# A convolution stem's forward and backward pass: every engine's order of work read from a fixed list

## The chip, the cores and the metric

The kernel runs on one core of a Trainium2 chip. A core has five engines that run at the same time, each in its own strict order of instructions: PE (TensorE, the matmuls; PEld are its weight loads), DVE (VectorE), ACT (ScalarE), POOL (GpSimd) and SP (SyncE, which here issues the transfers between HBM and on-chip memory). Sixteen DMA engines carry those transfers. An instruction starts when the one before it on its engine lets it and when the semaphores it waits for have come. The metric is device time in microseconds (us) of one execution; lower is better.

## What is computed

```python
def _fwd_reference(x, w, gn_gamma, gn_beta):     # x 2x16000x256, w 31x256x256
    s = 2
    L = (T - K) // s + 1                          # 7985
    h = jnp.einsum('blc,cd->bld', x[:, 0:s * L:s, :], w[0])
    for i in range(1, K):
        h = h + jnp.einsum('blc,cd->bld', x[:, i:i + s * L:s, :], w[i])
    mu = jnp.einsum('bld->bd', h)[:, None, :] / L
    var = jnp.einsum('bld->bd', (h - mu) ** 2)[:, None, :] / L
    h = (h - mu) / jnp.sqrt(var + 1e-5)
    h = h * gn_gamma[None, None, :] + gn_beta[None, None, :]
    return _gelu(h)

def reference(x, w, gn_gamma, gn_beta, grad_out):
    _out, _vjp = jax.vjp(_f, x, w, gn_gamma, gn_beta)
    return (_out, *_vjp(grad_out))
```

So it is a 31-tap convolution of stride 2 over 256 channels, a normalisation over time for each channel, a gelu, and then the gradients with respect to x, w, gamma and beta. All arrays are bf16.

## The kernel before

**Three convolutions as matmuls.** The forward pass (about 4 to 390 us, `f_mm`, line 815), the gradient of x (about 390 to 819 us, `g_mm`, line 1363) and the gradient of w (about 820 us to the end, `w_mm`, line 1653) are each a convolution. Each is made with fewer multiplications by splitting the taps and the positions into three branches, called A, B_ and C_ in the code, at several levels: DVE forms sums and differences of inputs and weights (`w_sub` 768, `tt` 783 and 1326, `w_add` 1616, `w_two` 1607, `pair_d` 1712), PE multiplies them, and ACT and DVE take the results out of PSUM and join them (`keep` 868, `f_evac` 890, `f_join` 917, `g_join` 1405, `w_sum` 1659). PSUM is a ring of four tiles, `ps0` to `ps3`, so a group of matmuls cannot begin in a tile until ACT or DVE has emptied it.

**Stages.** The forward pass goes over 2 batches (b) of 4 chunks (c) of time, and in each over the branches B_, A, C_. A chunk's x is brought in transposed into the one tile `XT` by four transfers (`x_load`, 713; the first chunk also through PE, `x_first`). Its h goes into the one tile `HS` (`f_evac`), and from there to HBM in one store of 1 MB (line 914). The elementwise part (normalisation, gelu, its derivative) runs under the matmuls of the second batch and of the first chunk of the x gradient. In the x gradient, DVE also forms differences of the gradient for the last stage (`d2_piece`, 1533), which go out to HBM and come back in the weight gradient (`d_tile`, 1641). That last stage has nine rounds n = 0 to 8; each takes four tiles of x (`x_tile`, 1625, through `x_raw`, 1618), two of differences (`D2`), forms `pair_x`, `leaf_d` and `pair_d` on DVE, and multiplies.

**What sets the order.** The program is not emitted as it is written. Every operation is recorded by `plan.add` with its engine, its assumed duration, its inputs and outputs, and is given a number in the order of recording; 3164 operations are recorded (900 groups of matmuls on PE, 994 on DVE, 721 on ACT, 23 on POOL, 526 transfers on SP). `Plan.order` then works out one list of all numbers, by due times taken backwards from the matmuls, a table of corrections by kind of operation (`self.lead`), and two rounds of a simulated run (`listing`, `latest`). `Plan.emit` (516) emits the operations in that list's order, and the framework keeps that order on every engine and puts in the semaphores. All transfers of more than 4 KB go through the one queue of SP (`load`, 602; `turn`, 612, for transposing ones). SP waits for what a transfer needs before it issues it, and what stands behind it on SP waits too.

**Tiles that the change moves.** In odd rounds of the weight gradient the four x tiles lie in `XT_` (line 1579), in even ones in `XS_`. `pair_x` and others take two tiles of the two batches as one operand through `both` (1598) where they lie near enough.

Of the kernel before, what the change touches and what calls it, by code (L numbers as in the profile page):

```python
# [37 lines left out]

class Plan:
# [3 lines left out]
    def __init__(self, tc):  # L43
# [10 lines left out]
        self.lead = {  # L54
            "F0 conv_stem_kernel wrapper": 5.6,
            "F0 f_evac last": -3.2,
            "F0 f_join f_evac": -10.3,
            "F0 f_join split": 14.0,
            "F0 f_mm f_three_ac": -0.4,
            "F0 f_mm f_three_b": 1.0,  # L60
            "F0 f_three_b split": -3.7,
            "F0 keep f_evac": -3.1,
            "F0 keep split": -17.8,
            "F0 load conv_stem_kernel": 58.4,
            "F0 load f_evac": -14.0,
            "F0 load put": 0.6,
            "F0 load x_pre": 3.5,
            "F0 load_gb conv_stem_kernel": -25.1,
            "F0 tt f_sums": -15.0,
            "F0 tt second": 4.0,  # L70
            "F0 tt third": -5.9,
            "F0 turn w2_part": -0.5,
            "F0 turn x_load": -4.6,
            "F0 w_sub w2_part": -5.7,
            "F0 x_pre conv_stem_kernel": 1.3,
            "F0 zero conv_stem_kernel": 0.9,
            "F0 zero f_evac": -7.8,
            "F0 zero w2_part": -33.8,
            "F0 zero x_load": -111.5,
            "F0a f_evac last": -19.8,  # L80
            "F0a f_join f_evac": 0.7,
            "F0a f_join f_first": -11.0,
            "F0a f_join split": 28.3,
            "F0a f_mm f_leaf": -8.4,
            "F0a f_mm f_three_ac": 0.2,
            "F0a f_mm f_three_b": -5.0,
            "F0a f_mm pe_turn": -48.4,
            "F0a f_three_b f_first": -12.7,
            "F0a f_three_b split": -30.8,
            "F0a keep f_first": -31.2,  # L90
            "F0a keep split": -10.0,
            "F0a load load_w": 58.4,
            "F0a load x_load": 82.3,
            "F0a load x_pre": 55.5,
            "F0a put x_first": -19.2,
            "F0a tt f_sums": -12.3,
            "F0a tt second": -19.7,
            "F0a tt third": -13.9,
            "F0a turn x_load": -48.2,
            "F0a w_sub f_first": -12.5,  # L100
            "F0a x_pre conv_stem_kernel": 13.3,
            "F0a zero load_w": 14.3,
            "F1 f_evac last": 4.0,
            "F1 f_join f_evac": 11.4,
            "F1 f_mm f_leaf": 0.7,
            "F1 f_mm f_three_b": 1.8,
            "F1 f_three_b plain": -0.7,
            "F1 f_three_b split": -2.0,
            "F1 gelu_batch conv_stem_kernel": -6.7,
            "F1 gelu_unit gelu_batch": 0.7,  # L110
            "F1 keep f_evac": -0.4,
            "F1 keep plain": -0.3,
            "F1 keep split": -34.2,
            "F1 load f_evac": 0.5,
            "F1 load gelu_unit": 3.0,
            "F1 load out0_store": -3.7,
            "F1 tiny elem_finalize": -260.7,
            "F1 tiny fwd_stats": 2.5,
            "F1 tt f_sums": -15.6,
            "F1 tt second": -1.3,  # L120
            "F1 tt third": 0.6,
            "F1 turn gelu_batch": 0.5,
            "F1 turn gelu_unit": 3.7,
            "F1 turn x_load": 1.8,
            "F1 zero gelu_batch": -52.4,
            "F1z f_evac last": -7.1,
            "F1z f_join f_evac": -5.3,
            "F1z f_join split": -17.5,
            "F1z f_mm f_leaf": -2.5,
            "F1z f_mm f_three_ac": 0.6,  # L130
            "F1z f_mm f_three_b": -0.3,
            "F1z f_three_b split": 2.4,
            "F1z keep f_evac": 7.0,
            "F1z keep split": -160.7,
            "F1z load f_evac": 7.0,
            "F1z tt f_sums": -20.3,
            "F1z tt second": -3.1,
            "F1z tt third": -0.7,
            "F1z turn x_load": 8.8,
            "F1z w_sub f_again": -0.3,  # L140
            "F1z zero f_evac": -10.2,
            "F1z zero x_load": -6.0,
            "G0 e_add e_comp": 3.6,
            "G0 e_comp conv_stem_kernel": -3.2,
            "G0 e_spread conv_stem_kernel": 8.2,
            "G0 g_join last": 1.0,
            "G0 g_mm g_leaf": -0.9,
            "G0 g_mm g_three_ac": 0.8,
            "G0 g_mm g_three_b": 0.7,
            "G0 g_three_b plain": 1.3,  # L150
            "G0 g_three_b split": 5.1,
            "G0 keep last": 1.4,
            "G0 keep plain": 4.1,
            "G0 keep split": -156.4,
            "G0 load dn_turn": 15.0,
            "G0 load e_load": -6.2,
            "G0 spread e_spread": -288.3,
            "G0 tt first": -2.4,
            "G0 tt outer": 17.1,
            "G0 tt second": -7.8,  # L160
            "G0 tt third": 14.0,
            "G0 turn dn_turn": -10.7,
            "G0 zero e_comp": -37.5,
            "G0 zero e_spread": 69.3,
            "G0a e_add e_comp": -0.5,
            "G0a e_comp conv_stem_kernel": -5.0,
            "G0a e_spread conv_stem_kernel": -1.4,
            "G0a g_join last": -0.9,
            "G0a g_mm g_leaf": 1.6,
            "G0a g_mm g_three_ac": 2.7,  # L170
            "G0a g_mm g_three_b": 2.3,
            "G0a g_three_b plain": 0.6,
            "G0a gelu_batch conv_stem_kernel": -22.1,
            "G0a gelu_unit gelu_batch": 0.3,
            "G0a keep last": 3.8,
            "G0a keep plain": -2.4,
            "G0a load dgb_store": 91.4,
            "G0a load dn_turn": -2.4,
            "G0a load e_load": 11.2,
            "G0a load g_store": 9.1,  # L180
            "G0a load gelu_unit": 4.5,
            "G0a load load_w2": -6.9,
            "G0a spread e_spread": -45.7,
            "G0a tiny elem_finalize": -2.2,
            "G0a tiny fwd_stats": -186.8,
            "G0a tt first": 20.5,
            "G0a tt gelu_unit": -0.6,
            "G0a tt second": -4.2,
            "G0a tt third": 1.7,
            "G0a turn dgb_store": -3.7,  # L190
            "G0a turn gelu_batch": -1.8,
            "G0a w_sub w2_sub": 2.0,
            "G0a zero conv_stem_kernel": -104.8,
            "G0a zero e_spread": -148.7,
            "G0a zero gelu_batch": -5.4,
            "G1 e_add e_comp": -0.5,
            "G1 e_comp conv_stem_kernel": 1.5,
            "G1 e_spread conv_stem_kernel": 0.2,
            "G1 g_join last": 1.0,
            "G1 g_join split": 4.3,  # L200
            "G1 g_mm g_three_ac": -2.1,
            "G1 g_mm g_three_b": -0.3,
            "G1 g_three_b split": -150.3,
            "G1 keep last": -1.0,
            "G1 keep split": 1.0,
            "G1 load d2_piece": 0.8,
            "G1 load dn_turn": -4.2,
            "G1 load e_load": -1.5,
            "G1 spread e_spread": 0.2,
            "G1 sub d2_piece": 0.3,  # L210
            "G1 tt first": 2.1,
            "G1 tt outer": 6.2,
            "G1 tt second": 7.7,
            "G1 tt third": 8.8,
            "G1 turn dn_turn": 0.4,
            "G1 zero e_comp": -0.2,
            "G1 zero e_spread": -0.6,
            "G1z g_join last": -4.0,
            "G1z g_join split": -7.1,
            "G1z g_mm g_three_b": 4.9,  # L220
            "G1z g_three_b split": 5.3,
            "G1z keep split": 7.7,
            "G1z load g_store": 15.8,
            "G1z tt first": -1.8,
            "G1z tt outer": 23.1,
            "G1z tt second": -0.8,
            "G1z tt third": -0.3,
            "W keep w_done": -6.2,
            "W keep weight_grad": -417.1,
            "W leaf_d weight_grad": -3.3,  # L230
            "W load d_tile": 1.3,
            "W load w_done": -3.6,
            "W load w_out": 16.2,
            "W load weight_grad": -11.1,
# [96 lines left out]
    def order(self):  # L331
# [3 lines left out]
        for i, o in enumerate(ops):  # L335
            for p in o["preds"]:
                succ[p].append(i)
# [1591 lines left out]
```

## Time and profile before

| what | us |
|---|---|
| median of 3 runs | 1110.25 |
| the three runs | 1110.12, 1110.25, 1116.37 |
| the profiled execution, its own time | 1114.1 |
| its span, first to last instruction | 1112.1 |
| first matmul starts | 4.49 |

The profile is of one execution. Its own time is 1114.1 us, 2.0 us more than its span, and 3.85 us above the median of the runs. "Waits" tells how long an engine sat idle and which instruction ended that idle time; a line number there is that of a helper, so many operations share one. The timeline merges neighbouring instructions of one line: its columns are start, duration, engine, line, operation, output and input, count, and in brackets the idle time before it. The table of stretches gives for each engine the busy time and the number of instructions in a stretch, the granted PE clock, the mean busy share of the DMA engines and GB/s.

### The profile page before, as it was taken

What the parts mean: (1) busy time and instruction counts of PE and PEld (TensorE: products, weight loads), DVE (VectorE), ACT (ScalarE), POOL (GpSimd) and SP (SyncE); (2) the same over time, 40 slices, a digit from 0 to 9 for tenths busy, and PEclk for the clock granted to TensorE, in tenths of its full rate; (3) what the DMA queues carried; (4) which work ended last, traced back from release to release, by engine and by line L of the source; (5) the groups of instructions that cost most, each with busy time, mean ns of one, the idle gap of its engine ahead of it and who ended that gap; (6) DMA issues with size and microseconds to landing.
All of it is one profiled execution on the core that took longest, in us unless ns stands there. A gap on an engine that the chain in (4) does not pass through costs nothing. (4 is left out here: it accounts for less than half of the span.)

```text
span 1112.1 us, 19739 instructions
## 1 busy us (share of the span) xinstructions
PE 1082.7 (97%) x8132; PEld 796.3 (72%) x8132; DVE 993.1 (89%) x1026; ACT 609.6 (55%) x854; POOL 11.0 (1%) x27
## 2 busy tenths in 40 slices
PE   5999999999999999999999998999999999999998
PEld 4888889988888984444444443444468888888887
DVE  6995958789998997999999979979689989999996
ACT  2253434588887659797866766665642323322332
POOL 0000000000000000000000000000000000000000
PEclk9999999999999999999999999999999999999999
DMA  9589999976969799889775999999789555796883
GB/s 227 66 220 225 242 272 272 253 151 167 190 202 186 204 334 313 203 254 276 191 245 159 280 330 295 289 301 311 247 277 270 181 194 146 262 333 205 277 255 101
DMA packets 346893, 261.47 MB, mean 235 GB/s; under 512 B 187702, under 2 KB 315572, under 8 KB 340916
## 3 DMA queue, kind: packets, MB, share of 16 engines
q1 hardware_dynamic: 346612, 260.22, 83.8%
q8 instruction: 63, 1.03, 0.4%
q14 instruction: 26, 0.21, 0.1%
q0 software_dynamic: 192, 0.00, 0.0%
HBM read 120.00 MB, written 94.86 MB: 193 GB/s over the span
## 5 line engine op out<-in xcount | busy, mean ns | idle before, releaser
L815 PE MATMUL ps<-arena 128*128 128x256 bf16 (+3 forms) x3668 | 397.7, 272 | 14.6 <-DMA arena<-in_x_dram 6.2
L1363 PE MATMUL ps<-arena 128*128 128x512 bf16 (+1 forms) x1872 | 401.0, 376 | 6.3 <-ACT arena L868 6.1
L815 PEld LDWEIGHTS <-arena 128*128 128x128 bf16 x3668 | 359.9, 99 | 52.2 <-DMA arena<-in_x_dram 6.4
L1363 PEld LDWEIGHTS <-arena 128*128 128x128 bf16 x1872 | 183.2, 98 | 223.8 <-issue 8.9
L868 ACT ACTIVATE arena<-ps 128x1024 bf16<-128x1024 f32 x189 | 191.7, 1022 | 238.8 <-PE ps L1653 123.2
L1653 PE MATMUL ps<-arena 128*128 128x256 bf16 x2592 | 284.2, 273 | 4.3 <-DVE arena L1607 4.3
L1653 PEld LDWEIGHTS <-arena 128*128 128x128 bf16 x2592 | 253.2, 98 | 35.5 <-DVE arena L1607 5.0
L783 DVE TENSOR_TENSOR arena<-arena 128x2064 bf16<-128x2064 bf16 (+7 forms) x132 | 164.7, 1270 | 24.6 <-PE ps L815 19.1
L1607 DVE TENSOR_TENSOR arena<-arena 128x4096 bf16<-128x4096 bf16 (+2 forms) x50 | 107.5, 2178 | 2.7 <-DMA arena<-d2d 2.7
L1167 DVE TENSOR_TENSOR arena<-arena 128x2048 bf16<-128x2048 bf16 (+1 forms) x80 | 95.6, 1198 | 8.9 <-ACT arena L1159 4.6
L1326 DVE TENSOR_TENSOR arena<-arena 128x1032 bf16<-128x1032 bf16 (+7 forms) x111 | 86.4, 803 | 6.7 <-PE ps L1363 5.1
L1390 ACT ACTIVATE ps<-ps 128x512 f32<-128x512 f32 x108 | 63.1, 587 | 34.8 <-PE ps L1363 34.6
L1616 DVE TENSOR_TENSOR arena<-arena 128x4096 bf16<-128x4096 bf16 x32 | 72.6, 2296 | 5.4 <-DMA arena<-in_x_dram 4.0
L1155 ACT ACTIVATE arena<-arena,stats 128x1024 bf16<-128x1024 bf16 (+1 forms) x64 | 75.1, 1209 | 0.8 <-DVE stats L1101 0.8
L1405 DVE TENSOR_TENSOR arena<-arena 128x1024 bf16<-128x1024 bf16 (+1 forms) x70 | 63.3, 919 | 7.1 <-ACT arena L868 7.0
L1549 DVE TENSOR_TENSOR arena<-arena 128x1536 bf16<-128x1536 bf16 (+3 forms) x56 | 61.9, 1128 | 8.0 <-DMA d2d<-arena 5.4
L844 ACT ACTIVATE ps<-ps 128x512 f32<-128x512 f32 x59 | 34.4, 583 | 62.1 <-PE ps L815 62.0
L1725 ACT COPY ps<-ps 128x512 f32<-128x512 f32 x54 | 30.8, 570 | 64.9 <-PE ps L1653 64.9
L1712 DVE TENSOR_TENSOR arena<-arena 128x2048 bf16<-128x2048 bf16 x54 | 64.8, 1232 | 1.1 <-DMA arena<-d2d 1.1
L768 DVE TENSOR_TENSOR arena<-arena 128x2048 bf16<-128x2048 bf16 (+1 forms) x45 | 50.8, 1151 | 16.4 <-DMA arena<-in_w_dram 9.6
L890 ACT ACTIVATE arena<-ps 128x512 bf16<-128x512 f32 (+1 forms) x64 | 36.8, 582 | 37.5 <-PE ps L815 27.7
L1659 DVE TENSOR_TENSOR arena<-arena 128x1024 bf16<-128x1024 bf16 x75 | 49.6, 699 | 6.8 <-ACT arena L868 6.8
(68 smaller groups left out, 464.3 us busy)
## 6 DMA issues: line engine op xcount, KB each, us to landing
arena<-in_x_dram SPq DMA_DIRECT2D x28, 1024.0 KB, 9.5
arena<-d2d SPq DMA_DIRECT2D x16, 1216.0 KB, 8.1
out_dram<-arena SPq DMA_DIRECT2D x35, 512.0 KB, 4.6
d2d<-arena SPq DMA_DIRECT2D x30, 384.0 KB, 6.2
arena<-dnd SPq DMA_DIRECT2D x10, 960.0 KB, 6.4
arena<-vl SPq DMA_DIRECT2D x9, 1024.0 KB, 12.2
arena<-in_x_dram SPq DMA_DIRECT2D x32, 256.0 KB, 4.4
hd<-arena SPq DMA_DIRECT2D x8, 1024.0 KB, 5.6
```

What stands on the lines that cost most here:

```text
L783: lambda: nc.vector.tensor_tensor(out=o, in0=a, in1=b, op=ALU.add))
L815: yield nc.tensor.matmul(ps[:, dh, cs], lhsT=wt, rhs=mv, start=s0, stop=False, skip_group_check=True)
L868: lambda: nc.scalar.activation(out=out, in_=ps, func=ACT.Copy, scale=scale))
L1155: lambda o=o, func=func, i=h[:, dh], sc=sc, bi=bi: SC.activation(out=o, in_=i, func=func, bias=bi, scale=sc))
L1167: add("DVE", dve(8 * wd), [o], [a, b_], lambda: V.tensor_tensor(out=o, in0=a, in1=b_, op=op))
L1326: lambda: nc.vector.tensor_tensor(out=o, in0=a, in1=b, op=ALU.add))
L1363: yield nc.tensor.matmul(ps[:, e, 0:wide], lhsT=lt, rhs=mv, start=s0, stop=False, skip_group_check=True)
L1405: add("DVE", dve(o.free_size(), rate), [o], [a, b], lambda: nc.vector.tensor_tensor(out=o, in0=a, in1=b, op=op))
L1607: add("DVE", dve(o.free_size()), outs, ins, lambda: nc.vector.tensor_tensor(out=o, in0=a, in1=b, op=op), kind=kind + " weight_grad")
L1616: add("DVE", dve(4096), [o], [a, b], lambda: nc.vector.tensor_tensor(out=o, in0=a, in1=b, op=ALU.add))
L1653: yield nc.tensor.matmul(ps[:, s, c0:c1], lhsT=lt, rhs=mv, start=s0, stop=False, skip_group_check=True)
L1712: add("DVE", dve(2048), [d4], [d], lambda: nc.vector.tensor_tensor(out=d4, in0=fan(d[:, o0:o0 + 3 * s + 1:s, :], 1, (o1 - o0) * D), in1=fa ...
```

## The change

No operation is added, removed or resized. Three things are different.

1. `Plan.order` no longer works anything out: it reads the list `STEPS`, whose running sum gives the operations' numbers in the order of emission (1, 7, 12, 6, 8, 22, 0, 9, ...). The table of corrections and the simulated run are gone.
2. The second and third of the four tiles of `XT_` change places, so that the two batches' tiles of one kind, (0, 1) with (1, 1) and (0, 0) with (1, 0), lie side by side.
3. What the planner records of dependences is a little coarser for operands of more than two strides, and a two-tile operand is recorded as one. With a fixed list this has no part in the order.

```diff
@@ -34,6 +34,85 @@
+STEPS = (
+    "1 6 5 -6 2 14 -22 9 1 -5 8 -11 22 -20 -1 23 -15 14 -2 13 -5 1 -5 6 2 -6 10 1 1 -7 13 -32 27 -4 -1 11 -5 -29 30 1 1 5 -2 -21 22 10 -30 -14 36 11 -46 "
...
+)
@@ class Plan @@
-        self.lead = {
-            "F0 conv_stem_kernel wrapper": 5.6,
...
-        }
     def order(self):
-        ops = self.ops
-        n = len(ops)
...
-        self.listing(due, succ)
-        for _ in range(self.rounds):
-            due = [d - self.lead.get(o["kind"], 0.0) for d, o in zip(self.latest(succ), ops)]
-            self.listing(due, succ)
-        return sorted(range(n), key=lambda i: (self.start[i], i))
+        steps = [int(x) for x in "".join(STEPS).split()]
+        out, at = [], 0
+        for d in steps:
+            at += d
+            out.append(at)
+        assert sorted(out) == list(range(len(self.ops)))
+        return out
...
-    XT_ = [sb(o, 8, 512) for o in (24576, 32768, 40960, 49152)]
+    XT_ = [sb(o, 8, 512) for o in (24576, 40960, 32768, 49152)]
...
-            one(both(outs), both(as_), both(bs), list(outs), ins)
+            o, a, b = (both(v) for v in (outs, as_, bs))
+            one(o, a, b, [o], [a, b])
```

Set against the order before, the list gives this (a place is an operation's rank on its own engine):

| engine | operations | at another place | moved by 5 or more | farthest |
|---|---|---|---|---|
| PE | 900 | 619 | 113 | 10 |
| DVE | 994 | 854 | 213 | 44 |
| ACT | 721 | 520 | 75 | 21 |
| POOL | 23 | 4 | 0 | 1 |
| SP | 526 | 429 | 73 | 38 |

The moves that are spoken of below, with the number of the operation, and its places before and after:

| operation | engine | what it is | place before | place after |
|---|---|---|---|---|
| 14, 15 | SP | weight loads of the first difference | 3, 4 | 10, 9 |
| 24, 26, 25, 23, 27, 29 | SP | other weight loads | 6, 11, 7, 5, 8, 10 | 2, 3, 5, 6, 7, 8 |
| 57 | DVE | the first difference of weights (`f_first`, 1015) | 7 | 11 |
| 84, 85, 86, 87, 94 | PE | leaf matmuls of the first branch, and the next group | 20, 22, 24, 28, 27 | 19, 20, 21, 22, 23 |
| 88 | PE | `f_three_b` of the first branch | 19 | 24 |
| 64, 81, 80 | DVE | sums of x for the first branch | 11, 9, 12 | 21, 23, 24 |
| 355 | SP | store of h of chunk (0, 1), 1 MB | 98 | 78 |
| 327, 352 | DVE | the joins that it waits for | 102, 104 | 97, 96 |
| 414, 415 | ACT | first writes of the next h into the same tile | 69, 70 | 68, 69 |
| 452 | PE | the group that needs the PSUM tile they empty | 148 | 139 |
| 2084 | ACT | `keep` that empties ps0 in the x gradient | 491 | 485 |
| 2208, 2210, 2211 | ACT | `e_spread` copies | 488, 489, 490 | 491, 493, 496 |
| 2457, 2472 | ACT, PE | `keep` that empties ps1, and the group that needs it | 575, 683 | 577, 687 |
| 2762, 2763 | SP | `D2` tiles of a round of the weight gradient | 447, 448 | 444, 445 |
| 2580, 2581, 2579 | SP | x tiles of the first round of the weight gradient, 1 MB each | 371, 380, 408 | 390, 418, 414 |
| 2582 | SP | the fourth of them | 424 | 424 |

More of the change, by code (lines that the diff above doesn't have):

```diff
@@ L290, in cells @@
         unit = 2048 if ap.space == bass.MemoryType.PSUM else 32
+        runs = []
+        for d in dims:
+            if runs and runs[-1][0] == d[0] * d[1]:
+                runs[-1] = [d[0], runs[-1][1] * d[1]]
+            else:
+                runs.append(list(d))
+        if len(runs) > 2:
+            lo = off + sum(min(0, d[0]) * (d[1] - 1) for d in runs)
+            hi = off + sum(max(0, d[0]) * (d[1] - 1) for d in runs)
+            return [(name, c) for c in range(lo * es // unit, (hi * es + es - 1) // unit + 1)]
         starts = [off]
@@ L300, in cells, with add @@
         return [(name, c) for c in out]
-    def add(self, eng, dur, outs, ins, fn, dma=None, slack=None, ns=28.0, tp=112.0, kind=None):
+    def add(self, eng, dur, outs, ins, fn, dma=None, slack=None, ns=28.0, tp=112.0, kind=None, lat=1.3):
         i = len(self.ops)
@@ L331, in order @@
     def order(self):
-        ops = self.ops
-        n = len(ops)
-        succ = [[] for _ in range(n)]
-        for i, o in enumerate(ops):
-            for p in o["preds"]:
-                succ[p].append(i)
-        due = [0.0] * n
-        for i in range(n - 1, -1, -1):
-            o = ops[i]
-            full = o["dur"] + (1.3 * o["dma"] + 6.0 if o["dma"] is not None else 0.15)
-            end = o["at"] if o["eng"] == "PE" else o["at"] + o["slack"]
-            for s in succ[i]:
-                end = min(end, due[s])
-            due[i] = end - full - self.lead.get(o["kind"], 0.0)
@@ L346, in order @@
-        self.listing(due, succ)
-        for _ in range(self.rounds):
-            due = [d - self.lead.get(o["kind"], 0.0) for d, o in zip(self.latest(succ), ops)]
-            self.listing(due, succ)
-        return sorted(range(n), key=lambda i: (self.start[i], i))
-    def latest(self, succ):
-        ops, n = self.ops, len(self.ops)
-        end = queue = max(self.ends)
-        late, due = [end] * n, [0.0] * n
-        left = [len(s) for s in succ]
-        wait = {e: [] for e in ("PE", "DVE", "ACT", "POOL", "SP")}
-        free = {e: end for e in wait}
-        for i in range(n):
-            if not left[i]:
-                wait[ops[i]["eng"]].append(i)
-        for _ in range(n):
-            best = None
-            for e, w in wait.items():
-                if w:
-                    t = max(min(late[i], free[e]) for i in w)
-                    if best is None or t > best[0]:
-                        best = (t, e, w)
-            t, e, w = best
-            i = max((i for i in w if min(late[i], free[e]) >= t - 1e-9), key=lambda i: self.start[i])
-            w.remove(i)
-            o = ops[i]
-            if o["dma"] is not None:
-                queue = min(late[i] - 0.9, queue) - o["dma"] * 1.3
-                t = min(queue - 1.3 - 1.0, free[e])
-            else:
-                t = min(late[i], free[e])
-            due[i] = t - o["dur"]
-            free[e] = due[i] + self.overlap.get(e, 0.0)
-            for p in sorted(o["preds"]):
-                q = ops[p]
-                lag = (0.0 if e == "PE" else 0.034) if q["eng"] == e and q["dma"] is None else 0.12
-                if e != "PE" and q["eng"] == "PE":
-                    lag += 0.2
-                late[p] = min(late[p], due[i] - lag)
-                left[p] -= 1
-                if not left[p]:
-                    wait[q["eng"]].append(p)
-        return due
@@ L608, in load @@
         ns = (PKS if out.space == bass.MemoryType.DRAM else PK)[pk]
-        add(eng, {"POOL": 0.74, "SP": 0.25 + 0.0005 * np_, "ACT": 0.4}[eng], [out], [in_],
+        add(eng, {"POOL": 0.74, "SP": 0.47 + 0.00012 * np_, "ACT": 0.4}[eng], [out], [in_],
             lambda: e.dma_start(out=out, in_=in_), dma=np_ * ns / 16e3 * 1.03, ns=ns, tp=SH[pk], slack=slack)
@@ L613, in turn @@
         np_ = nbytes / 256
-        add("SP", 0.15 + 0.00105 * np_, [out], [in_],
-            lambda: nc.sync.dma_start_transpose(out=out, in_=in_), dma=np_ * PK[256] / 16e3 * 1.03, ns=PK[256], tp=SH[256], slack=slack)
+        t = np_ * PK[256] / 16e3 * 1.03
+        add("SP", max(1.3, 0.15 + 0.00105 * np_), [out], [in_],
+            lambda: nc.sync.dma_start_transpose(out=out, in_=in_), dma=t, ns=PK[256], tp=SH[256], slack=slack,
+            lat=0.3 - 0.5 * max(0.0, t - 0.6))
     def zero(out, n, eng="POOL"):
@@ L1845, in conv_stem_kernel @@
         if (b, c, br) == (1, 0, B_):
-            plan.stage = "F1"
+            stage, plan.stage = plan.stage, "Ea0"
             fwd_stats(0)
-            for _ in gelu_batch(0, GT[0], *PACE[0]):
-                pass
+            for c_, e in gelu_batch(0, GT[0], *PACE[0]):
+                plan.stage = f"Ea{c_ + e}"
             plan.slack = PACE[0][0] + 16 * PACE[0][1]
@@ L1872, in conv_stem_kernel @@
             if (b, c) == (0, 0):
-                for _ in ge:
-                    pass
+                plan.stage = "Eb0"
+                for c_, e in ge:
+                    plan.stage = f"Eb{c_ + e}"
                 plan.slack = PACE[1][0] + 16 * PACE[1][1]
@@ L1890, in conv_stem_kernel @@
                 d2_piece(1, pc)
-    plan.stage = "W"
+    plan.stage = "W0"
     weight_grad()
```

354 lines of the change are left out of this document (9 added, 345 removed), and 74 rows, old and new, of the table STEPS.

## Prediction

> **What bounds the kernel now.** I read the page's first part, then PE's waits. PE is busy 97% of the span, DVE 89%, and the number of matmuls does not change, so an order can win only what PE idles. The first fence is the page's head; the second is PE's waits: engine and line, what ended the idle time, total us, times, longest.
>
> ```profile
> span 1112.1 us, 19739 instructions
> PE 1082.7 (97%) x8132; PEld 796.3 (72%) x8132; DVE 993.1 (89%) x1026; ACT 609.6 (55%) x854; POOL 11.0 (1%) x27
> ```
>
> ```profile
> PE ps L815 <- DMA arena<-in_x_dram: 6.2, 2, 4.5
> PE ps L1363 <- ACT arena L868: 6.1, 4, 3.8
> PE ps L1653 <- DVE arena L1607: 4.3, 7, 1.0
> PE ps L815 <- DVE arena L768: 2.6, 1, 2.6
> PE ps L815 <- ACT arena L728: 2.3, 1, 2.3
> PE ps L815 <- ACT arena L890: 2.0, 1, 2.0
> PE ps L815 <- DVE arena L783: 1.5, 1, 1.5
> ```
>
> The idle time is 25.0 us. The first row is the first x tiles' arrival, and 2.6, 2.3 and 1.5 are also of the first 24 us. What lies behind them is 6.1 + 4.3 + 2.0 = 12.4 us. So the most that an order can take is 12.4 us, and 6.4 us more if the start had no wait but for x. I take the terms one by one and sum them against the profiled execution's own 1114.1 us.
>
> **Term 1, the start.** First PE's timeline, then DVE's, then SP's, then stretches of line 815 (stretch: length, PE busy and count, PEld, clock, DMA share, GB/s).
>
> ```profile
> 8.06 2.41 PE L815 MATMUL ps<-arena 128*128 128x128 bf16 x32 [1.68 <-DMA arena<-in_x_dram]
> 12.79 0.37 PE L815 MATMUL ps<-arena 128*128 128x256 bf16 x1 [2.32 <-ACT arena L728]
> 14.67 3.36 PE L815 MATMUL ps<-arena 128*128 128x256 bf16 x15 [1.51 <-DVE arena L783]
> 20.64 10.59 PE L815 MATMUL ps<-arena 128*128 128x256 bf16 x69 [2.60 <-DVE arena L768]
> ```
>
> ```profile
> 10.14 0.69 DVE L768 TENSOR_TENSOR arena<-arena 128x1024 bf16<-128x1024 bf16 x1 [8.58 <-DMA arena<-in_w_dram]
> 16.97 12.16 DVE L768 TENSOR_TENSOR arena<-arena 128x2048 bf16<-128x2048 bf16 x11
> ```
>
> ```profile
> 2.85 14.58 SPq L610 DMA_DIRECT2D arena<-in_w_dram  x16
> ```
>
> ```profile
> 12.79:16.10 3.31, 1.79 (x8) 1.09 (x8) 1.00 1.22 290
> 20.64:24.00 3.36, 3.36 (x16) 2.36 (x17) 1.00 1.22 187
> 27.00:30.50 3.50, 3.50 (x34) 3.12 (x32) 1.00 0.00 0
> ```
>
> In the old order 1 + 15 + 69 = 85 matmuls of 256 columns are done at 20.64 + 10.59 = 31.2 us. The list puts six weight loads, five of 256 KB and one of 192 KB (1.51 MB), ahead of loads 14 and 15. At 290 GB/s that is 5.2 us, so difference 57, which began at 10.14, begins at 15.3 and ends at 16.0, and the first leaf matmul runs at 16.1, not 12.8: 3.3 us lost there. But then 84 to 87 follow without 88 between them. The first 16 take 3.4 us (16 in 3.36), to 19.5; 84 and 85 need the difference of the next two loads, which DVE reaches at 19.8 after two others of 1.1 us (11 in 12.16) and a wait for load 30, and run to 23.2 at the same rate. 86 and 87 need the last loads: 3.54 MB behind 14 and 15 in the old order, 12.2 us after 10.1, so 22.3, plus 1.2 for the difference: 23.5. Their 32 matmuls at 0.10 us (34 in 3.50) end at 26.9; 94 needs three more differences, 26.8, and ends at 28.6. 64 + 16 = 80 are done, and 85 at 29.2. The start gains **2.0 us**. The bounds: a loss of 3.3 if the later first matmul is not made up, a gain of 6.4 if all three waits went. I take 2.0, because the last load, which bounds both orders, leaves no more.
>
> **Term 2, the wait at 161 us.** Four rows of the timelines of DVE, SP, ACT and PE.
>
> ```profile
> 133.25 0.69 DVE L917 TENSOR_TENSOR arena<-arena 128x1024 bf16<-128x1024 bf16 x1
> 153.29 0.43 SPq L610 DMA_DIRECT2D hd<-arena  x1
> 160.22 0.60 ACT L890 ACTIVATE arena<-ps 128x512 bf16<-128x512 f32 x1 [3.07 <-DMA hd<-arena]
> 161.54 6.67 PE L815 MATMUL ps<-arena 128*128 128x256 bf16 x62 [1.99 <-ACT arena L890]
> ```
>
> The tile of h was ready at 133.9 (the join 352), but its store 355 was issued at 153.3, behind 20 other transfers, and let ACT go at 160.2, 6.9 us later. ACT then emptied the PSUM tile that PE's 452 needed. The list moves the store 20 places up and its joins 5 and 8. Even with the joins at their old time it lands at 133.9 + 6.9 = 140.8, 17 us before 158. So the wait goes: **2.0 us**. What is queued behind: SP now waits at the store for the joins, with x transposes of the next chunk behind it; they have the 27 us between 133.9 and 161 for some 22 us of issuing. Next late there would be those transposes.
>
> **Term 3, two waits in the x gradient.** ACT and PE near 680, then near 772.
>
> ```profile
> 677.93 1.57 ACT L1299 COPY arena<-arena 128x768 bf16<-128x768 bf16 x2
> 679.40 2.84 ACT L868 ACTIVATE arena<-ps 128x1024 bf16<-128x1024 f32 x3
> 680.47 2.85 PE L1363 MATMUL ps<-arena 128*128 128x512 bf16 x12 [3.75 <-ACT arena L868]
> ```
>
> ```profile
> 771.21 1.02 ACT L868 ACTIVATE arena<-ps 128x1024 bf16<-128x1024 f32 x1 [3.98 <-DMA out_dram<-arena]
> 772.29 4.04 PE L1363 MATMUL ps<-arena 128*128 128x512 bf16 x18 [1.36 <-ACT arena L868]
> ```
>
> At 679.4 `keep` 2084 stood behind three e_spread copies that had waited for DVE; the list puts it ahead of all three, and its matmuls five groups earlier. The whole **3.75 us** go. At 772 ACT waited for a store of the x gradient; the list puts PE's group four places later, 4 x 0.22 x 4 = 3.5 us of other matmuls (18 in 4.04, four a group), more than the wait: **1.36 us** go. The other 6.1 - 3.75 - 1.36 = 1.0 us I leave standing: their groups move two and three places, of which I cannot say that it suffices.
>
> **Term 4, the weight gradient.** DVE's timeline at its largest gap, and two stretches (PE, PEld, DVE, ACT, POOL busy, clock, DMA share, GB/s).
>
> ```profile
> 901.82 5.03 DVE L1607 TENSOR_TENSOR arena<-arena 128x4608 bf16<-128x4608 bf16 x2 [2.68 <-DMA arena<-d2d]
> ```
>
> ```profile
> 640.00:700.00 60.00, 55.31 (x257) 24.93 (x255) 50.27 (x59) 36.41 (x52) 0.00 (x0) 1.00 1.03 320
> 780.00:800.00 20.00, 20.00 (x95) 9.20 (x94) 14.86 (x16) 12.17 (x17) 0.00 (x0) 1.00 0.69 223
> 840.00:1075.00 235.00, 232.13 (x2123) 207.10 (x2120) 228.88 (x168) 70.28 (x88) 0.00 (x0) 1.00 0.72 231
> ```
>
> Here DVE is as full as PE (228.88 of 235 us), so a late tile on DVE becomes a wait of PE later: the 4.3 us. The list issues the two D2 tiles 2762 and 2763 three places earlier, ahead of a 1 MB x tile (3.3 us at 320 GB/s), more than the gap of 2.68. I take **2.7 us**; the bounds are 0 and 4.3. The exchange of the two XT_ tiles I cost at nothing: both sums of a round need all four tiles before any pair does, so no load or add waits for another tile by it; no wait in the rows above is of that kind. Bounds 0 and 1 us a side, the size of one such wait (longest 1.0).
>
> **Sum.** 1114.1 - 2.0 - 2.0 - 3.75 - 1.36 - 2.7 = **1102.3 us**. The profiled execution lies 3.85 us above the median of 1110.25; I take nothing off for that, as late landings of the kind removed are likely what it had more of. Against the median it is -0.7%.
>
> A rule to weigh: the row at 680.47 shows 12 matmuls of 512 columns in 2.85 us behind a pause of 3.75, which is no half rate. The Trainium skill, "TensorE: Matmul & The Clock Gate", Part 1: The HAM clock gate, says that PE drops to half its clock after an idle window of about 3.4 us. By that rule the wait at 680 had cost some 1.7 us more (an estimate: half of one window) and the sum would be 1100.6; the trace does not agree for this pause, though the halves at the start (16 in 3.36 against 34 in 3.50) fit it while the clock column says 1.00 for both.
>
> **Rivals.** *All waits go:* behind the start nothing is left, 1114.1 - 12.4 - 2.0 = 1099.7, and with the start's 6.4 in place of 2.0, 1095.3. For it: each long wait has a move that answers it. Against it: landings scatter between executions.
>
> *The weight gradient takes the gain back.* The rows: SP, DVE and PE at its entrance.
>
> ```profile
> 803.34 0.60 SPq L610 DMA_DIRECT2D arena<-in_x_dram  x1
> 811.79 2.29 DVE L1616 TENSOR_TENSOR arena<-arena 128x4096 bf16<-128x4096 bf16 x1 [2.96 <-DMA arena<-in_x_dram]
> 815.14 2.29 DVE L1607 TENSOR_TENSOR arena<-arena 128x4096 bf16<-128x4096 bf16 x1
> 819.81 12.39 PE L1653 MATMUL ps<-arena 128*128 128x256 bf16 x112 [0.30 <-DVE arena L1607]
> ```
>
> PE's first group there needs the pair ready at 815.14 + 2.29 = 817.4, so only 2.4 us of margin. If DVE's part does not move with PE, terms 1 to 3 (9.1 us) shrink to 2.4, and 1114.1 - 2.4 - 2.7 = 1109.0. Against it: load 2582 waits at 803.34 for a matmul of the x gradient, so it comes earlier with PE.
>
> *The other side, slower: the x tiles moved into a full stretch.*
>
> ```profile
> 719.08 0.69 SPq L610 DMA_DIRECT2D arena<-in_x_dram  x1
> 774.06 0.62 SPq L610 DMA_DIRECT2D arena<-in_x_dram  x1
> ```
>
> These two and a third between them, 3 MB, go 19, 6 and 38 places back on SP, towards 751 to 791. At 320 GB/s they are 9.8 us. If they land behind the last d2 pieces and on the path to that first pair, the time is up to 1102.3 + 9.8 = 1112.1. It decides once 8.0 of the 9.8 us are exposed (1110.25 - 1102.3). Against it: at 780 to 800 the DMA share is 0.69, room for 6.2 us; for it: the stretch before has 1.03. The Trainium skill, "DMA: Bandwidth & Descriptors", Where 436 GB/s comes from, puts HBM's limit for a core at about 358 GB/s; by that, 320 is not full, and the exposure would be smaller. No run here shows 358.
>
> *It does nothing new:* other landings are late in place of these, and it stays near 1110.
>
> **How the numbers follow.** A measurement of this kernel tells about 1% from no change, so faster means under 1099.1 and slower over 1121.4. Forecast (1099 to 1107) 0.45; all waits go (under 1099) 0.27; gain taken back or nothing new (1107 to 1111) 0.15; x tiles late or a new wait (over 1111) 0.13, of which 0.05 over 1121.4. Faster 0.27, same 0.68, slower 0.05. The range runs from 1095.5, all waits gone, to 1111, most of the x tiles exposed.
>
> **What would show it.** Right: no PE wait over 1 us between 24 and 819 us; 85 matmuls done near 29 us; the h store issued before 135; `keep` ahead of the copies near 675; no 2.7 us gap of DVE near 890. Wrong: a PE wait over 2 us at the weight gradient's entrance for DVE's pair, or new waits for a PSUM tile in the forward pass at places that had none.

## The result, and the profile after

| | us |
|---|---|
| before, median of 4 runs | 1112.72 (1110.12 to 1116.37) |
| after, median of 4 runs | 1100.93 (1100.32 to 1101.5) |
| ratio after to before, 95% interval | 0.9884 (0.986 to 0.9907) |
| the profiled execution after: own time, span | 1101.5, 1099.5 |

A fourth run of the kernel before, 1115.19, has come to the three that stand ahead of the prediction. The change makes the kernel 1.2% faster; 1100.93 lies 1.4 us under the forecast of 1102.3. From profile to profile the spans differ by 1112.1 - 1099.5 = 12.6 us. The first fence is the engines' row of the page after, the second PE's waits (line numbers have moved: 509 is `f_mm`, 1057 `g_mm`, 1348 `w_mm`, 462 `w_sub`, 477 `tt`, 562 `keep`, 1301 `w_two`, 1407 `pair_d`; in most kernels of the experiments they are one less).

```profile
PE 1078.2 (98%) x8132; PEld 794.9 (72%) x8132; DVE 995.2 (91%) x1026; ACT 610.5 (56%) x854; POOL 10.3 (1%) x27
```

```profile
PE ps L509 <- DVE arena L462: 7.1, 3, 5.2
PE ps L509 <- DMA arena<-in_x_dram: 6.3, 2, 4.5
PE ps L1348 <- DVE arena L1301: 2.1, 1, 2.1
PE ps L1348 <- DVE arena L1407: 0.8, 1, 0.8
PE ps L509 <- DVE arena L477: 0.3, 1, 0.3
PE ps L1057 <- ACT ps L1084: 0.3, 1, 0.3
PE ps L1057 <- ACT arena L562: 0.3, 1, 0.3
```

The first two rows are the start. Of the 12.4 us that lay behind it, 0.3 + 0.3 + 0.3 + 2.1 + 0.8 = 3.8 us are left, and no pause between 24 and 819 us is longer than 0.4 us. The first matmul of the x gradient and the first of the weight gradient cut the span into its three convolutions. The fences show PE's timeline there, before and then after (the last row of a timeline ends with the window that was asked for, so its count is not the whole run of matmuls).

```profile
412.15 231.74 PE L1363 MATMUL ps<-arena 128*128 128x512 bf16 x1084
...
819.81 10.42 PE L1653 MATMUL ps<-arena 128*128 128x256 bf16 x94 [0.30 <-DVE arena L1607]
```

```profile
408.52 22.86 PE L1057 MATMUL ps<-arena 128*128 128x512 bf16 x104
...
809.02 21.23 PE L1348 MATMUL ps<-arena 128*128 128x256 bf16 x193
```

The forward pass became 412.15 - 408.52 = 3.6 us shorter, the x gradient (407.66 to 400.50) 7.2, and the weight gradient up to the span's end (292.29 to 290.48) 1.8. The matmuls of the forward pass and of the x gradient on the two pages, before and then after (count, busy us, mean ns, idle us in front of them):

```profile
L815 PE MATMUL ps<-arena 128*128 128x256 bf16 (+3 forms) x3668 | 397.7, 272 | 14.6 <-DMA arena<-in_x_dram 6.2
L1363 PE MATMUL ps<-arena 128*128 128x512 bf16 (+1 forms) x1872 | 401.0, 376 | 6.3 <-ACT arena L868 6.1
```

```profile
L509 PE MATMUL ps<-arena 128*128 128x256 bf16 (+3 forms) x3668 | 394.9, 271 | 13.7 <-DVE arena L462 7.1
L1057 PE MATMUL ps<-arena 128*128 128x512 bf16 (+1 forms) x1872 | 400.0, 376 | 0.6 <-ACT ps L1084 0.3
```

The x gradient's 1872 matmuls are now busy 400.0 us of 400.5, so nothing is left there for an order to win. The rows also show that the waits are not all of the gain. With the weight gradient (4.3 before, 2.9 after) PE's idle time fell from 25.2 to 17.2, by 8.0 us; its busy time, for the same 8132 matmuls, fell from 1082.7 to 1078.2, by 4.5 us, and 2.8 of these lie in the forward pass. The start, PE's timeline:

```profile
15.86 3.60 PE L509 MATMUL ps<-arena 128*128 128x256 bf16 x16 [5.24 <-DVE arena L462]
19.82 1.93 PE L509 MATMUL ps<-arena 128*128 128x256 bf16 x16 [0.36 <-DVE arena L462]
23.22 22.00 PE L509 MATMUL ps<-arena 128*128 128x256 bf16 x199 [1.48 <-DVE arena L462]
```

Sixteen matmuls of 256 columns take 3.60 us at 15.86, half rate, and 1.93 us at 19.82, full rate. In the two traces 44 such matmuls run at half rate at the start before and 16 after. At (3.60 - 1.93) / 16 = 0.10 us each, the 28 are some 2.9 us (an estimate from these rows), about what the forward pass lost in busy time. PE's waits in the first 24 us did not shrink: 12.6 us before, 13.4 after.

And the stretches that answer to those shown of before: the end of the x gradient and the weight gradient.

```profile
780.00:800.00 20.00, 20.00 (x97) 9.25 (x95) 13.68 (x14) 12.67 (x17) 0.00 (x0) 1.00 0.84 268
...
840.00:1075.00 235.00, 232.14 (x2125) 207.47 (x2124) 233.44 (x173) 69.50 (x89) 0.53 (x1) 1.00 0.70 228
```

The DMA share at 780 to 800 rose from 0.69 to 0.84. Of the three moved x tiles one was issued in that stretch, at 785.0 (the others at 742.2 and 774.5), and the whole schedule is some 11 us earlier there, so the two rows do not show the tiles alone. DVE is now busy 233.44 of 235 us in the weight gradient, and PE still idles as much there between 840 and 1075 (232.14 against 232.13): the D2 gap of DVE is gone, but one long wait of PE at 1000.91 has come in.

### The profile page after: what moved, and what is told of

Same layout as the page of the kernel before. It is cut to its first block, busy times and chain, and to the rows that moved or that the text cites. A ratio compares the mean times of both kernels' runs of the same rounds, so it can differ in the third digit from the quotient of the medians.

```text
span 1099.5 us, 19714 instructions
## 1 busy us (share of the span) xinstructions
PE 1078.2 (98%) x8132; PEld 794.9 (72%) x8132; DVE 995.2 (91%) x1026; ACT 610.5 (56%) x854; POOL 10.3 (1%) x27
## 5 line engine op out<-in xcount | busy, mean ns | idle before, releaser
L477 DVE TENSOR_TENSOR arena<-arena 128x2064 bf16<-128x2064 bf16 (+8 forms) x132 | 164.1, 1266 | 22.2 <-PE ps L509 19.6
L462 DVE TENSOR_TENSOR arena<-arena 128x2048 bf16<-128x2048 bf16 (+1 forms) x45 | 51.0, 1147 | 13.4 <-DMA arena<-in_w_dram 10.8
```

The costliest lines, as they stand in the source:

```text
L477: lambda: nc.vector.tensor_tensor(out=o, in0=a, in1=b, op=ALU.add))
```

## The experiments

Each kernel is the changed one with another list. In the diffs `old` is the order that the planner of the kernel before had worked out, as numbers of operations, `new` is the order in `STEPS`. A ratio is to the kernel before, timed on the same chip in the same five rounds, with its 95% interval; one thousandth is 1.1 us. The microseconds behind a ratio are worked out from it, and the difference of the two medians can be up to 1.7 us off them.

**Is it the order, and nothing else?**

```diff
-order = new
+order = old
```

> The changed kernel with the old order written out as its list; the exchanged x tiles and everything else of the change stay. If the order alone makes the difference (my theory): as slow as the kernel before, ratio to it 0.997 to 1.003, with the PE waits at the x gradient's keep and at 161 us back. If the places of the x tiles or the coarser dependences made it: near 0.989.

Measured: 1114.82 against 1114.83 us, ratio 1.0003 (0.9987 to 1.002). The exchange in `XT_`, the coarser dependences and the missing planner do nothing to the time with the old order that two thousandths would show; the gain is the list. The other way round, the new list with the exchange undone:

```diff
-    XT_ = [sb(o, 8, 512) for o in (24576, 40960, 32768, 49152)]
+    XT_ = [sb(o, 8, 512) for o in (24576, 32768, 40960, 49152)]
```

> The changed kernel with the four x tiles back in their old places, the list kept. Theory: no load or add waits for another tile by it, so the same 1100.3 to 1101.5 us. Rival: the neighbouring places take false waits away, and without them 2 us or more of new DVE or PE waits stand in the weight gradient.

Measured: 1102.73, ratio 0.9898 (0.9876 to 0.992), whose interval holds the 0.9884 of the change, and its PE waits behind the start are the same. The exchange is worth nothing that can be seen. Its profile has one thing of its own: behind the wait of 2.08 us at 1000.64, where the profile after has one of 2.07, PE ran 22 matmuls of 256 columns in 4 us at a clock of 0.57, against 37 at 1.00, and the same 864 matmuls took 96.16 us against 94.49.

**The start alone, and the weight gradient alone.** The first 110 operations in the new order, the rest in the old:

```diff
-order = new
+order = new[:110] + [j for j in old if j not in new[:110]]
```

> The first 110 operations in the new order (to about 31 us), the rest in the old one. Theory: 85 matmuls of 256 columns are done near 29.1 us in place of 31.2, and the time is 2 us under the old list's. Rival: what follows in the old order waits for DVE or the loads and nothing is kept at 160 us.

Measured: 1112.6 against 1114.83, ratio 0.998 (0.9967 to 0.9993): 2.2 us, with an interval from 0.8 to 3.7. Its PE timeline has the start of the new list:

```profile
23.25 16.86 PE L508 MATMUL ps<-arena 128*128 128x256 bf16 x152 [1.03 <-DVE arena L461]
```

85 matmuls of 256 columns are done at 29.3 us, as expected. But the old start is seldom as late as in the profile of before. In the seven profiles with the old start they are done at 31.2 (before) and at 29.0 to 30.3 (the six others); in the seven with the new start, at 28.8 to 29.5. The means are 29.7 and 29.1. So the start is worth some 0.6 us (an estimate from these means); where the rest of this kernel's 2.2 us comes from is not shown. The half rate goes the same way: 31 to 44 matmuls with the old start, 16 to 26 with the new.

The old order up to the first matmul group of the weight gradient (place 2588 of the list), the new behind it:

```diff
-order = new
+order = old[:2588] + [j for j in new if j not in old[:2588]]
```

> The old order up to the first group of the weight gradient, the new one behind it. Theory: 2 to 3 us under the old list's time, with DVE's gap of 2.7 us near 902 gone and the wait of 2.07 us that the new order has in its sixth round there too. Rival: DVE is the bound there and no order helps, 0 us.

Measured: 1112.6 against 1114.83, ratio 0.9985 (0.9967 to 1.0002): 1.7 us, just not told from none, and under the 2 to 3 expected.

**The prediction's single moves.** `keep` 2084 ahead of the three `e_spread` copies on ACT:

```diff
 ACT, places 488 on
-2208, 2210, 2211, 2084, 2098, 2090
+2084, 2208, 2210, 2211, 2098, 2090
```

> The old order with one change: on ACT, the keep 2084 that empties ps0 stands ahead of the three e_spread copies 2208, 2210 and 2211. Theory: the pause of 3.6 to 3.8 us at 680 goes, and with it the half clock that the old order showed behind it in three of four profiles (6 to 15 matmuls at 0.43 us in place of 0.22, 1.3 to 3.2 us); so 4 to 6 us under the old list's 1114.8, near 1110, with a smaller scatter. Rival: DVE or a transfer stands behind it at 772 or at the weight gradient's entrance, and under 2 us are kept.

Measured: 1115.06 against 1115.0, ratio 1.0001 (0.9983 to 1.0019). Nothing. PE's timeline and ACT's of that kernel:

```profile
681.13 19.03 PE L1056 MATMUL ps<-arena 128*128 128x512 bf16 x78 [2.77 <-ACT arena L561]
...
774.57 5.77 PE L1056 MATMUL ps<-arena 128*128 128x512 bf16 x26 [2.67 <-ACT arena L561]
```

```profile
674.95 1.02 ACT L561 ACTIVATE arena<-ps 128x1024 bf16<-128x1024 f32 x1 [1.14 <-PE ps L1056]
678.35 0.22 ACT L987 COPY arena<-arena 128x28 bf16<-128x28 bf16 x1 [2.38 <-DVE arena L1019]
678.60 1.56 ACT L992 COPY arena<-arena 128x768 bf16<-128x768 bf16 x2
680.07 1.93 ACT L561 ACTIVATE arena<-ps 128x1024 bf16<-128x1024 f32 x2
```

2084 is done at 676.0, as the prediction had it, but the next `keep`, 2098, still stands behind the copies, which wait for DVE; it runs at 680.07, and PE's next group needs it. The wait shrinks from 3.75 to 2.77, and the one near 772 grows from 1.36 to 2.67. The new list has all three `keep` (2084, 2098, 2090) ahead of the copies.

The store of h behind its last join, 13 places up on SP:

```diff
 SP
-place 98: 355
+place 85: 355
```

> The old order with one change: on SP, the store 355 of h of chunk (0,1) stands right behind its last join, 13 places up. Theory: it lands near 141, the wait of 2.0 to 2.5 us at 161 goes, and 2 us are kept: near 1112.6. Rival: the x transposes or weight transposes behind it come later and PE waits for them at 137 to 165 instead, 0 us.

Measured: 1114.01 against 1115.0, ratio 0.9998 (0.998 to 1.0017). The wait at 161 is gone, and others stand in its place. PE's timeline, then DVE's, then SP's last x transpose of that chunk, and the same transpose in the kernel before and after the change:

```profile
99.83 71.87 PE L508 MATMUL ps<-arena 128*128 128x256 bf16 x662
173.03 4.17 PE L508 MATMUL ps<-arena 128*128 128x256 bf16 x40 [1.33 <-DVE arena L476]
177.38 38.81 PE L508 MATMUL ps<-arena 128*128 128x231 bf16 x380 [0.19 <-DVE arena L476]
216.80 13.42 PE L508 MATMUL ps<-arena 128*128 128x256 bf16 x121 [0.61 <-DVE arena L476]
```

```profile
169.09 0.69 DVE L386 TENSOR_TENSOR arena<-arena 128x1024 bf16<-128x1024 bf16 x1 [1.28 <-DMA arena<-in_x_dram]
```

```profile
132.07 0.34 SPq L301 DMA_DIRECT2D hd<-arena  x1
...
150.13 4.86 SPq L307 DMA_TRANSPOSE arena<-in_x_dram  x1
```

```profile
148.06 3.58 SPq L615 DMA_TRANSPOSE arena<-in_x_dram  x1
```

```profile
120.37 0.33 SPq L302 DMA_DIRECT2D hd<-arena  x1
...
141.50 4.06 SPq L308 DMA_TRANSPOSE arena<-in_x_dram  x1
```

With the store moved alone, the last transpose's issue ends at 155.0 instead of 151.6. The plain loads of x behind it (for `x_pre`, line 386) go out from 157.1 instead of 155.0; DVE waits for one of those, and PE for DVE. The new list has the joins and the transposes earlier too: the store goes out at 120.4, the transpose is issued by 145.6.

All four of the prediction's moves at once (the start, the store, `keep` 2084, and the D2 tiles 2762 and 2763 ahead of x tile 2759):

```diff
-order = new
+order = new[:110] + [j for j in old if j not in new[:110]]
+2208, 2210, 2211 behind 2084; 355 behind 352; 2759 behind 2763
```

> The old order with four of the list's moves and nothing else: the first 110 operations, the store 355, the keep 2084, and the D2 tiles 2762 and 2763 ahead of the x tile 2759. Theory, these moves are the change: the terms add up, 1114.8 - 2.1 - 2.2 - 5 - 2.7, near 1103. Rival: the many small moves between them hold the gain, and with four alone new waits appear, over 1107.

Measured: 1114.01 against 1115.0, ratio 0.9992 (0.9972 to 1.0013). So the four moves are not what the list is worth; not even the start's 2.2 us can be seen here. DVE's gap of 2.68 us for a D2 tile at 902 is gone in this profile, but one of 1.81 us for another stands at 973, and the weight gradient lasts 1114.2 - 821.95 = 292.2 us, as before (292.3). PE's waits in the x gradient are now five, 9.3 us in all, against 6.1 in four before:

```profile
PE ps L1056 <- ACT arena L561: 9.3, 5, 3.4
```

**Whole stages.** The whole change is worth 0.0116 of 1114.8, 12.9 us; the start's 2.2 and the weight gradient's 1.7 leave some 9 without an owner. The new order in the x gradient only, and then up to the x gradient only:

```diff
-order = new
+head = old[:1212] + [j for j in new if j not in old[:1212]]
+order = head[:2588] + [j for j in old if j not in head[:2588]]
```

> The old list up to the first matmul of the x gradient (place 1212) and from the end of it (place 2588), the new list's order for what lies between. All the rest of the change is kept. The whole change is worth -13.8 us, the start alone -2.2 and the weight gradient alone -1.7, so some 10 us have no owner. Theory A (the x gradient's order as a whole owns them): 1114.8 - 8 to - 10, so 1105 to 1107, ratio 0.991 to 0.993, with no PE wait above 1 us between 400 and 819 us. Theory B (the forward pass's order owns them, by handing the x gradient an earlier and steadier state): under 2 us less, 1113 to 1115, waits for ACT near 680 and 772 still there.

```diff
-order = new
+order = new[:1214] + [j for j in old if j not in new[:1214]]
```

> The new list up to the first matmul of the x gradient (place 1214), the old order behind it. Theory A (x gradient owns the rest): the start's 2.2 us, and the 2 us of the wait at 161 handed back at the waits near 680 and 772: 1111 to 1113, ratio 0.997 to 0.999. Theory B (the forward pass owns the rest): 1103 to 1106, ratio 0.990 to 0.992, and the two waits in the x gradient gone or under 1 us. Sum without anything handed back: 1114.8 - 2.2 - 2.0 = 1110.6, ratio 0.996.

Measured, against 1114.72: the x gradient 1107.04, ratio 0.9935 (0.9915 to 0.9954), 7.3 us less; the forward pass 1110.45, ratio 0.9966 (0.9951 to 0.9981), 3.8 us less. With the weight gradient's 0.9985 the three ratios miss 1 by 0.0065 + 0.0034 + 0.0015 = 0.0114, and the whole change by 0.0116. By stages the gains add up, as far as intervals of some 0.002 a side can tell; forward pass only came out where its expectation put the sum without anything handed back (1110.6). The other kernels' profiles agree, read as above (first matmul of the x gradient, first of the weight gradient):

| kernel | x gradient begins | its length | order in the x gradient |
|---|---|---|---|
| before | 412.15 | 407.7 | old |
| old list | 412.19 | 407.4 | old |
| `keep` 2084 first | 413.94 | 407.8 | old, one move |
| store early | 411.36 | 409.6 | old |
| four moves | 409.93 | 412.0 | old, one move |
| forward pass only | 408.05 | 407.1 | old |
| x gradient only | 409.03 | 400.2 | new |
| after | 408.52 | 400.5 | new |

With the old order the x gradient lasts 407 us or more wherever it begins (the kernels not in the table: 407.9 to 414.4), with the new one 400 to 402. Four microseconds won ahead of it stay won with the old order untouched (forward pass only); in the four moves' profile the 2.2 us won ahead of it are lost again in it, with the five waits shown. One profile is one execution: with the old forward order the x gradient began anywhere from 409.0 to 413.9.

**The x tiles.** The old list with the three x tiles at their later places, then the new list with them at the earlier ones:

```diff
 SP, old list
-2580 at 371, 2581 at 380, 2579 at 408
+2580 at 389, 2581 at 418, 2579 at 414
```

> The old list, with only the three x tiles of the first round of the weight gradient (2580, 2581, 2579; 1 MB each) issued at the places that the new list gives them (20, 38 and 6 places later). Theory T2 (the x gradient is short of DMA between 640 and 780 us, and these 3 MB are taken out of it): the wait near 772 goes or falls below 0.5 us, DMA share at 720 to 780 falls from about 0.95 to about 0.87 as with the new list, 1110 to 1113, ratio 0.996 to 0.998. Theory T3 (the order of ACT and PE does it): the waits near 680 and 772 stay as they are, 1114 to 1116, ratio 1.000. The prediction's rival (late tiles at the weight gradient's entrance): a PE wait of 2 to 10 us near 820, 1117 to 1122.

```diff
 SP, new list
-2580 at 390, 2581 at 418, 2579 at 414
+2580 at 371, 2581 at 385, 2579 at 408
```

> The new list, with only the same three x tiles issued at the places of the old list (2580 at 371, 2579 at 408, 2581 at 385, the earliest that the operations ahead of it allow). In the old list, the later places alone cost some 9 us. Theory U (the tiles' later places are part of what the new order of the x gradient wins, since its other transfers stand closer in their stead): slower than the new list by 2 us or more, 1103 to 1110, ratio 0.992 to 0.998, PE waits for ACT between 700 and 790 us. Theory V (the tiles' places win nothing, the order of the other operations does): 1099 to 1102, ratio 0.987 to 0.990, no PE wait above 1 us between 400 and 819 us.

Measured: late in the old list 1125.69 against 1114.72, ratio 1.0083 (1.0056 to 1.0111), some 9 us slower; early in the new list 1103.06 against 1113.7, ratio 0.9895 (0.9873 to 0.9917), not told from the 0.9884 of the change. DMA issues at 740 to 790 us of the old list, and then of the old list with the tiles late (name, engine, operation, count, KB each, median us to landing), with the timelines of SP, DVE, ACT and PE of the latter:

```profile
arena<-dnd SPq DMA_DIRECT2D x2, 960.0 KB, 6.5
```

```profile
arena<-dnd SPq DMA_DIRECT2D x2, 960.0 KB, 10.9
```

```profile
750.28 0.65 SPq L301 DMA_DIRECT2D arena<-in_x_dram  x1
750.98 0.70 SPq L301 DMA_DIRECT2D arena<-dnd  x1
...
754.64 10.91 SPq L301 DMA_DIRECT2D d2d<-arena  x4
```

```profile
762.05 2.90 DVE L1242 TENSOR_TENSOR arena<-arena 128x3584 bf16<-128x3584 bf16 x2 [5.73 <-DMA arena<-dnd]
```

```profile
774.99 1.02 ACT L561 ACTIVATE arena<-ps 128x1024 bf16<-128x1024 f32 x1 [6.20 <-DMA out_dram<-arena]
```

```profile
776.07 27.57 PE L1056 MATMUL ps<-arena 128*128 128x512 bf16 x128 [3.58 <-ACT arena L561]
```

An x tile of 1 MB now goes out 0.7 us ahead of a load that DVE needs for the d2 pieces. That load takes 10.9 us; the 6.5 is of the next load of its size, 11 us later in the old list. DVE waits 5.73 us for it, SP stands 10.91 us over the four pieces that DVE forms from it (6.08 in the old list), with the stores of the x gradient behind them, ACT waits 6.20 us for one of those stores, and PE 3.58 us for ACT. In this profile the x gradient lasts 414.4 us against 407.4. Its execution took 1119.25 us, one of the two fastest of six (the other four 1125.5 to 1127.8), so what the slower ones lost more is not shown. My theory that the later tiles relieve a stretch short of DMA gets no support: alone they cost 9 us, and in the new list their places make no difference that can be told (0.0011 between the ratios). In the new list what was next to them has moved too.

**Beyond the change.** The new list's longest wait behind the start, 2.07 us at 1000.91, is for pair 2954, which stands on DVE behind pair 2962 and sum 2921. It was moved ahead of both, and of the two stores of 2921's result on SP:

```diff
 DVE, new list, places 911 to 914
-2921, 2953, 2962, 2954
+2953, 2954, 2962, 2921
```

> The new list with one change: DVE's pair 2954, which PE waits 2.07 us for in the sixth round of the weight gradient, stands ahead of the single pair 2962 and the sum 2921 (with that sum's two stores behind it). Theory: 1.14 + 0.6 us of that wait go, 1.7 us under the new list, near 1099.2. Rival: DVE is full there and the same wait returns within the next rounds, 1100.9.

Measured: 1100.62, ratio 0.9877 (0.9854 to 0.99). PE's timeline there:

```profile
991.87 6.27 PE L1347 MATMUL ps<-arena 128*128 128x256 bf16 x56 [0.79 <-DVE arena L1406]
...
998.60 1.92 PE L1347 MATMUL ps<-arena 128*128 128x256 bf16 x16 [0.46 <-DVE arena L1300]
1001.47 93.03 PE L1347 MATMUL ps<-arena 128*128 128x256 bf16 x848 [0.95 <-ACT arena L561]
```

Two waits of 0.46 and 0.95 stand in place of one of 2.07; what is left of the gain is below what the rounds can tell.

## Why the prediction was right, and where it was not

The time and its sign came out: 11.8 us below the profiled execution were forecast, 12.6 were found. The way there came out in part only. By stage:

| stage | forecast | between the profiles | alone in its own kernel |
|---|---|---|---|
| forward pass (terms 1 and 2) | -4.0 | -3.6 | -3.8 |
| x gradient (term 3) | -5.1 | -7.2 | -7.3 |
| weight gradient (term 4) | -2.7 | -1.8 | -1.7 |

The stages miss by 0.4 too much, 2.1 too little and 0.9 too much. That the total misses by only 0.8 is in part luck.

**The bound.** "An order can win only what PE idles" does not hold: 4.5 of the 12.6 us are busy time. At the start the new order runs fewer matmuls at half rate; the 1.0 us in the x gradient and the 0.7 in the weight gradient were not taken apart.

**The basis.** Setting the sum against the profiled execution's 1114.1 and not against the median of three was right. In the later rounds the kernel before had medians of 1113.7 to 1115.0: the 1110.25 was the low draw.

**Term 1 (start, -2.0).** The new order's times came out: the first leaf matmul was put at 16.1 and ran at 15.86; 84 at 19.8, and it ran at 19.82; 86 at 23.5, and it ran at 23.22; 85 matmuls done at 29.2, and 32 + 53 of them were done at 23.22 + 53 x 22.00 / 199 = 29.1. One step between did not: the sixteen at 19.82 were put at half rate up to 23.2, ran at full rate up to 21.75, and PE then waited 1.48 us for the last difference; since the last loads bound the start, this cost nothing. The size was luck. It was set against 31.2 us of the one profile of before, and the other profiles of the old start have 29.0 to 30.3.

**Term 2 (161 us, -2.0).** The wait went, and the size is right. The reason given, the store's own place, does not hold up alone: much as the prediction feared in its last sentence on it, the transposes of the next chunk were later, and the x loads behind them were what PE waited for next. It is the forward order as a whole that wins; which of its moves do was not taken apart.

**Term 3 (x gradient).** This is the step that was off. "The whole 3.75 us go", for the one `keep` ahead of the copies, is wrong as a cause: moved alone it wins nothing, since the next `keep` stands behind the same copies. The 1.36 us near 772 are no fixed price either: with the old order of the x gradient that wait is 0.8 to 3.1 us from profile to profile, and 2.67 and 3.38 with `keep` 2084 first and with the four moves. And the sum was too small: it left 1.0 us of waits standing that went too, but for 0.5 us, and it had no term for PE's busy time (401.0 to 400.0). What exactly in that order carries the 7 us was not taken apart further than this: it is neither the first `keep` alone, nor the x tiles' places alone.

**Term 4.** The gap of DVE near 890 is gone; the size was 2.7 where the runs show 1.7 to 1.8. The reason given does not hold up alone here either: with the two D2 tiles moved and nothing else in the stage (four moves) the gap went, another came, and the stage stayed at 292.2 us. The new order has a wait of its own of 2.07 us for a pair, and taking that one away won nothing that can be told (0.9877 against 0.9884). What in the order shortens the stage was not taken apart.

**The exchange of the tiles**, costed at nothing, is nothing.

**The rivals.** *All waits go* was the nearest in kind: 3.8 of 12.4 us are left. *The weight gradient takes the gain back* did not happen: PE entered it 10.8 us sooner and waited for nothing, since the loads and DVE's pair moved with it. In the kernel with the new order in the x gradient alone, PE's timeline has, 14.5 us behind the entrance,

```profile
823.69 6.51 PE L1348 MATMUL ps<-arena 128*128 128x256 bf16 x58 [2.12 <-DVE arena L1301]
```

The old list has a wait of 1.71 us at that place without entering sooner, so this row does not show that anything was taken back.

*The x tiles in a full stretch* was priced at 9.8 us, and alone in the old list they cost 9; but not by landing late at the weight gradient's entrance. They delayed the load issued behind them. *It does nothing new* is what became of the store and of the `keep` when they were moved alone, and not of the list.

**The rule weighed.** The Trainium skill, "TensorE: Matmul & The Clock Gate", Part 1: The HAM clock gate, says that PE falls to half its clock after an idle window of about 3.4 us. The prediction found the trace not in agreement for the pause at 680. That was one draw. These are the 4 us behind the same pause (length, PE busy and matmuls, clock, DMA share, GB/s), in four kernels with the old order there, the last with its one move: before (pause 3.75 us), forward pass only (3.63), weight gradient only (3.79), `keep` 2084 first (2.77).

```profile
680.47:684.47 4.00, 4.00 (x19) 1.00 0.99 296
```

```profile
675.61:679.61 4.00, 4.00 (x19) 1.00 0.97 298
```

```profile
680.68:684.68 4.00, 4.00 (x10) 0.50 0.98 298
```

```profile
681.13:685.13 4.00, 4.00 (x12) 0.59 0.99 297
```

At full clock 19 matmuls run in 4 us, at half clock 10. So the gate does close behind such a pause in some executions and not in others. Its price is in PE's timeline, as the same 420 matmuls behind the pause, weight gradient only and then forward pass only:

```profile
680.68 92.74 PE L1056 MATMUL ps<-arena 128*128 128x512 bf16 x420 [3.79 <-ACT arena L561]
```

```profile
675.61 90.28 PE L1056 MATMUL ps<-arena 128*128 128x512 bf16 x420 [3.63 <-ACT arena L561]
```

That is 2.5 us on top of the pause. The profile of before happened to have none of it at 680, so that is not part of the 12.6 us; the half rate at the start is. Such a price may be part of why the kernel before spreads over 1109 to 1120 us in the rounds and the changed one over 1.2 us in four runs: the new order has no pause behind the start that is longer than 2.1 us. That was not tested, and two kernels speak against it as the whole reason: the new list with the exchange undone lost its clock behind a pause of 2.08 us, and the kernel with the new order in the x gradient alone, with no pause there over 2.2 us either, spreads over 5.0 us.

## What to carry to other kernels

A wait in a tightly ordered pipeline has an heir: moving the one instruction that a wait names wins nothing if the next user of the same queue or the same PSUM ring stands behind the same late thing, so look at what would be late next before costing a move at its whole wait. Here stages added up and single moves did not: test a reordered stage as a whole, and take how far its bounding engine is from being full as a bound and not as the gain. A forecast set against one profile inherits that execution's accidents, as the start did; a second profile of the same kernel shows which waits are always there. The big transfer moved in a full queue was paid for here by what was issued right behind it, not by its own reader.

## What the runs showed of the hardware that was not expected

The clock behind a pause is a matter of the execution and not of the pause's length alone: 3.63 and 3.75 us left PE at full clock, 2.77 us brought it to 0.59 over the next 4 us, 3.79 us to 0.50. A pause of 2.08 us brought it to 0.57 in the new list with the exchange undone, and the same pause of 2.07 us left it at 1.00 in the profile after. The Trainium skill, "TensorE: Matmul & The Clock Gate", Part 1: The HAM clock gate, says that the window runs free, which agrees with a chance outcome, while pauses of 2.08 and 2.77 us are shorter than its window of about 3.4 us.
